# Another table of positions for the attention steps of a fused attention and token-mixing kernel

## The chip, the cores and the metric

One core of a Trainium2 chip runs the whole kernel. The metric is the device time of one execution in microseconds (us); the number given for a kernel is the median of its runs.

## What is computed

The reference has two parts. In the first, for 8 batches and 8 heads, queries are pooled in pairs and attend to 1152 keys; the second mixes the result over tokens and channels:

```python
q_pool = q.reshape(B, H, S // 2, 2, D).mean(axis=3)
scores = scale * np.matmul(q_pool, k.transpose(0, 1, 3, 2))
scores = scores - np.max(scores, axis=-1, keepdims=True)
attn = np.exp(scores)
attn = attn / (np.sum(attn, axis=-1, keepdims=True) + 1e-09)
x = np.matmul(attn, v)            # heads side by side: [8, 576, 512]
theta = x @ w_theta
y = w_tok_r @ (x * cos(theta)) + w_tok_i @ (x * sin(theta))
u = x + y
return u + np.maximum(u @ w_ch, 0.0)
```

All arrays hold float32, the four weight matrices come as 64-bit floats and are taken apart in the kernel.

## The kernel before

The work has two phases. **Phase one** is attention. The 64 (batch, head) problems are done two heads at a time, in 32 *pairs*, numbered 0 to 31. **Phase two** is the mixing, batch by batch, and has an order of its own that the change leaves as it is.

A pair consists of some hundred *steps*, one `Op` each, made in `operations()`. By engine they are:

- SP (DMA issues): `load_q`, `load_k` (four each), `load_v`, `load_max` (six, ten for pair 0), and `norm_spread`, `norm_load`, `norm_save`, `norm_bcast`, `norm_store` for the row sums.
- POOL: `diff` (differences of neighbouring keys, L720) and `ss` (sums of the exponentials, L868).
- DVE: `pool_q` (L713), `t` (two transposes of the operands, L745 and L747; in pair 0 the TensorE does them), `lo` (low parts, L778), `mx` (15 maxima over PSUM, L803), `nm` and `nt` (the row maxima and their transpose, L815 and L818), and `norm_recip`, `norm_out`, `norm_turn` (L920, L944, L949).
- ACT: `hi` (high parts, L774), `rn` (rounds the maxima to `nmrr`, L836), `x` (18 exponentials, L861), `xu` and `sm` (L885, L905).
- PE: `pm` (15 score tiles for the maxima, L791), `e` (18 exact score tiles of three or four terms, L851), `av` (18 products with v, L873), `ns` (row sums, L894).

A step's name is followed here by its two indices, as in the table: `pm40` is the first of the three matmuls of query block 4, `e18` the ninth score tile of the second half of the queries, `av06` the product of the seventh tile of the first half.

What binds the steps is data and room. A block of maxima runs `pm40`, `mx40`, `pm41`, `mx41`, `pm42`, `mx42` in one slot of PSUM; chains of `e` and `x` (up to three tiles, each added onto the one before) hold a slot too; `t` holds one until its `lo` is done. There are four slots of two banks, and `av` and `ns` fill one of them by halves. Exponentials go into 14 buffers, given back once `av` and `ss` (or `ns`) have read them.

The order of all this is made ahead, by a list scheduler (`schedule`, from line 366) that runs on the host. Each step has a *position*, `PLACE[name] + 18 * pair`; entries with the prefix `p0:` replace it for pair 0. Each engine has one list, sorted by position. `ahead` says how many of its first steps may be started out of order: 24 on SP; `LOOK = 8` on the others while the first step in the list belongs to pair 0 or 1, or to the last pair; and one, so the plain sorted order, in all pairs between. Among those it may choose, `look` takes the first in sorted order unless a later one would be finished, by the planner's own durations, before the first could start (plus `slack`):

```python
edge = main[e] and (main[e][0].i < 2 or main[e][0].i >= NPAIRS - 1)
return LOOK if edge else 1
```

A step that has not been run yet, because it waits, keeps its place among the eight. The instructions of each engine are then issued in the order that was found, and on the chip each engine keeps that order.

Beside the pairs runs a second list, 18 weight jobs (`w_fetch` to `w_tlo`), whose position is `w0 + wd * job + wk * step`. On PE a step that needs another array mode than the one before is sorted as if it stood `turn` further back. `early` loads the first input of phase two, and `xhi` and `xlo` split it; `xt` and `th` stand for phase two's first matmuls and issue nothing.

Pair 0 has two sets of maxima: `nm00`, `nt00` and four `load_max` (numbers 0 to 3, L827) give the rows of the first half of the queries and lead over `rn` to its first score tile `e00`; `nm10`, `nt10` and `load_max` 4 to 9 (L827, L833) give the second half, which pair 0 reads from a tile of its own, `nmr_0u`.

Of the kernel before, what the change touches and what calls it, by code (L numbers as in the profile page):

```python
# [25 lines left out]
    "load_k00": -38.40059, "load_k10": -28.36788, "load_k20": -27.61457, "load_k30": -39.35929,  # L26
    "diff00": -32.80156, "diff10": -32.44173, "load_q00": -54.34104, "load_q10": -91.84454,
    "load_q20": -27.44506, "load_q30": -38.99972, "pool_q00": -29.15684, "t10": -22.00105,
    "hi10": -21.02379, "lo10": -20.04949, "t00": -22.18585, "hi00": -22.31522, "lo00": -21.74663,
    "pm40": -17.06847, "mx40": -16.83563, "pm30": -17.17711, "mx30": -18.87555, "pm41": -14.70191,  # L30
    "mx41": -15.31905, "pm31": -14.17544, "mx31": -15.19312, "pm42": -13.57796, "mx42": -15.06456,
    "pm32": -12.76746, "mx32": -14.97779, "pm10": -12.17304, "mx10": -13.89269, "pm00": -11.03266,
    "mx00": -13.56397, "pm11": -9.95283, "mx11": -13.12904, "pm01": -8.94236, "mx01": -12.84205,
    "pm12": -8.45123, "mx12": -12.18622, "pm02": -7.5643, "mx02": -11.83974, "pm20": -7.04275,
    "mx20": -11.61033, "pm21": -6.55952, "mx21": -11.06424, "pm22": -4.02978, "mx22": -9.22241,
    "nm00": -8.00188, "nt00": -6.38411, "load_max00": -24.4908, "load_max10": -24.14235,
    "load_max20": -8.92986, "load_max30": -19.40568, "load_max40": -118.57957,
    "load_max50": -8.27529, "e00": 4.11175, "x00": -1.62783, "e02": 4.64667, "x02": 0.31132,
    "e01": 5.19959, "e04": 5.23843, "x01": 0.32182, "x04": 0.70875, "ss01": 2.41792,
    "e03": 6.0347, "x03": 1.15614, "load_v00": -6.85969, "ss02": 5.42273, "e05": 8.75871,  # L40
    "ss03": 5.61781, "x05": 1.54237, "e06": 9.18085, "x06": 2.58909, "e10": 9.86331,
    "e07": 10.38561, "ss04": 5.9122, "x10": 2.72114, "x07": 2.81716, "e11": 10.43852,
    "e08": 11.21097, "x11": 3.45665, "ss05": 15.96989, "x08": 6.26382, "e13": 11.41578,
    "e12": 11.43369, "x13": 8.12539, "ss06": 16.1637, "x12": 8.88963, "e14": 11.69101,
    "e15": 12.02213, "x14": 11.71284, "av00": 12.31907, "x15": 9.74425, "e16": 15.17488,
    "e17": 15.17109, "av01": 13.07033, "ss11": 7.67054, "x16": 12.96257, "av02": 15.1759,
    "x17": 12.50312, "av10": 16.02034, "av03": 15.34448, "ss12": 8.07714, "av11": 16.18557,
    "av04": 15.38473, "av12": 16.56557, "ss13": 10.54574, "av05": 15.79164, "av13": 17.48058,
    "av06": 16.9326, "av14": 18.02337, "ss14": 11.31074, "av07": 17.89469, "av15": 19.02375,
    "av08": 20.38694, "ss15": 11.52553, "av16": 20.50752, "xu00": 16.19192, "e18": 18.22843,  # L50
    "ss16": 16.35297, "x18": 15.73589, "av17": 21.17044, "av18": 22.34946, "xu10": 17.1598,
    "ns00": 25.06113, "ns10": 25.1094, "ns20": 25.72144, "sm00": 19.45308,
    "norm_spread00": -21.70776, "norm_load00": 13.58894, "norm_recip00": 55.52903,
    "norm_save00": 61.28433, "norm_bcast00": 63.23545, "norm_bcast10": 57.24014,
    "norm_out00": 62.72609, "norm_store00": 31.66353, "norm_turn00": 69.51872,
    "norm_store10": 59.99388, "pool_q10": -107.14221, "ns30": 146.18829, "ns40": -13.08814,
# [1448 lines left out]
```

## Time and profile before

| | us |
|---|---|
| median of 3 runs | 1266.46 (1264.79 to 1267.41) |
| the profiled execution, whole time | 1265.34 |
| its span, first to last instruction | 1263.6 |
| PE busy | 1211.3 |
| DVE busy | 966.7 |
| POOL busy | 810.9 |
| ACT busy | 679.8 |

The span is what the trace shows; the profiled execution's own time is 1.74 us more, for what lies around it. Busy time is time in which an engine has an instruction running, and on PE matmuls overlap. Times in the rows below count from the span's start. Phase one fills the first 817 us or so.

### The profile page before, as it was taken

To read this page: it belongs to the slowest core of one execution; us is meant where nothing else is said; L and a number is where in the kernel's file an instruction comes from. 1 tells how busy PE (TensorE), PEld (TensorE's weight loads), DVE (VectorE), ACT (ScalarE), POOL (GpSimd) and SP (SyncE) were. 2 spreads that over 40 slices of the span, in tenths; PEclk is the share of its full clock that TensorE was granted. 3 is DMA by queue.
4 is the path that set the end of the run, shared out by engine and by line. 5 is a ranking of instruction groups with operands and counts; after the bars stand their busy time and mean duration, and the time that the engine had idled before them with its cause. 6 is when DMAs were issued, how large, how long until landed. Compare 5 with 4: busy or idle time off the path is not lost.

```text
span 1263.6 us, 27774 instructions
## 1 busy us (share of the span) xinstructions
PE 1211.3 (96%) x10915; PEld 946.4 (75%) x10915; DVE 966.7 (77%) x1313; ACT 679.8 (54%) x1129; POOL 810.9 (64%) x596
## 2 busy tenths in 40 slices
PE   3899999999999999999999999999999999999998
PEld 2567666666666766766666666698999999999998
DVE  6788989999888898988989886166675857658553
ACT  1466656656666765666666665464343433344430
POOL 1688988998987998898988888334333423242320
PEclk7899999999999999999999999999999999999999
DMA  6454555557555456455556431315545546455332
GB/s 122 80 105 94 115 102 121 125 124 168 100 86 109 101 107 124 85 101 102 117 98 111 105 68 40 97 34 151 120 110 114 124 110 135 103 121 115 86 52 38
DMA packets 489403, 130.16 MB, mean 103 GB/s; under 512 B 459576, under 2 KB 460280, under 8 KB 489272
## 3 DMA queue, kind: packets, MB, share of 16 engines
q1 hardware_dynamic: 489272, 128.39, 48.9%
q8 instruction: 85, 1.39, 0.5%
q14 instruction: 46, 0.38, 0.1%
HBM read 97.61 MB, written 29.52 MB: 101 GB/s over the span
## 4 chain that ended last, share of the span: by engine, by line
PE 80%; ACT 8%; DVE 6%; DMA 2%; issue 2%; POOL 1%; SPq 0%; ACTq 0%; DVEq 0%; POOLq 0%
PE b L873 23%; PE b L851 18%; PE py L1325 15%; PE b L791 7%; PE pr L1364 6%; ACT pc L861 6%; PE pth L1237 6%; PE b L894 4%; DVE mx L803 2%; DMA xT<-xd 1%; DVE kk L1261 1%; DMA dn<-rod 1%; ACT Z L1294 1%; DVE r L1263 1%; ACT kk L1259 1%
## 5 line engine op out<-in xcount | busy, mean ns | idle before, releaser
L803 DVE TENSOR_REDUCE mx<-b 128x2 f32<-128x768 f32 x480 | 440.3, 953 | 79.4 <-PE b L791 76.7
L868 POOL TENSOR_TENSOR ss<-ss,pc 128x576 f32<-128x576 f32 x314 | 448.7, 1436 | 19.6 <-ACT pc L861 2.6
L861 ACT ACTIVATE pc<-b 128x576 f32<-128x576 f32 x576 | 353.6, 652 | 184.5 <-PE b L851 156.6
L873 PE MATMUL b<-pc,vn 128*64 128x288 f32 x2304 | 306.3, 411 | 0.0
L873 PEld LDWEIGHTS b<-pc,vn 128*64 128x64 f32 x2304 | 154.5, 136 | 112.3 <-issue 17.8
L1325 PE MATMUL py<-wtk,Z 128*128 128x288 f32 x1728 | 234.0, 296 | 0.0
L1325 PEld LDWEIGHTS py<-wtk,Z 128*128 128x128 f32 x1728 | 232.2, 189 | 1.4 <-DVE uT L1341 0.2
L1298 POOL TENSOR_TENSOR Z<-ab,Z 128x512 fp32r<-128x512 f32 x40 | 53.3, 1333 | 266.3 <-ACT Z L1294 266.3
L851 PE MATMUL b<-hi 64*128 64x288 f32 x1152 | 187.1, 321 | 13.2 <-ACT pc L861 8.8
L791 PE MATMUL b<-hi 64*128 64x384 f32 x960 | 172.8, 379 | 14.8 <-DVE mx L803 8.5
L851 PE MATMUL b<-lo,hi 64*128 64x288 f32 x1152 | 170.6, 293 | 0.0
L851 PE MATMUL b<-hi,lo 64*128 64x288 f32 x1152 | 170.2, 292 | 0.0
L868 POOL TENSOR_TENSOR ss<-pc,pc 128x576 f32<-128x576 f32 x64 | 105.5, 1648 | 94.0 <-ACT pc L861 94.0
L851 PEld LDWEIGHTS b<-hi 64*128 64x128 f32 x1152 | 108.3, 185 | 52.8 <-ACT pc L861 33.9
L791 PEld LDWEIGHTS b<-hi 64*128 64x128 f32 x960 | 87.8, 188 | 80.1 <-DVE mx L803 51.9
L851 PEld LDWEIGHTS b<-lo,hi 64*128 64x128 f32 x1152 | 109.1, 186 | 0.0
L851 PEld LDWEIGHTS b<-hi,lo 64*128 64x128 f32 x1152 | 108.8, 185 | 0.0
L1364 PE MATMUL pr<-us,wch 128*128 128x288 f32 x768 | 106.6, 296 | 1.2 <-DVE uT L1377 1.2
L1364 PEld LDWEIGHTS pr<-us,wch 128*128 128x128 f32 x768 | 104.3, 188 | 3.8 <-DVE uT L1377 2.4
L720 POOL TENSOR_TENSOR qk<-qk 128x384 f32<-128x384 f32 x62 | 63.7, 1027 | 20.6 <-DMA qk<-in_k_dram 16.6
L1237 PE MATMUL pth<-wth,xh 128*128 128x512 f32 x288 | 72.9, 395 | 2.4 <-DVE r L1263 2.4
L774 ACT CAST hi<-b 128x768 fp32r<-128x768 f32 x64 | 56.0, 879 | 33.8 <-DVE b L745 23.5
(100 smaller groups left out, 1320.1 us busy)
## 6 DMA issues: line engine op xcount, KB each, us to landing
vn<-in_v_dram SPq DMA_DIRECT2D x32, 576.0 KB
qn<-in_q_dram SPq DMA_DIRECT2D x124, 144.0 KB
qk<-in_k_dram SPq DMA_DIRECT2D x124, 144.0 KB
xd<-xu SPq DMA_DIRECT2D x32, 288.0 KB
xT<-xd SPq DMA_DIRECT2D x8, 1152.0 KB
xn<-xbd SPq DMA_DIRECT2D x140, 64.0 KB
out_dram<-ub SPq DMA_DIRECT2D x124, 72.0 KB
xbd<-xb SPq DMA_DIRECT2D x28, 288.0 KB
```

What stands on the lines that cost most here:

```text
L720: (nc.vector if op.eng == DVE else nc.gpsimd).tensor_tensor(kn[:, c : c + W], kn[:, c : c + W], kn[:, c - W : c], ALU.subtract)
L774: nc.scalar.copy(hi, src)
L791: nc.tensor.matmul(pm[:, h, 0:W], hi[hs, q : q + P], hi[hs, group(g)], start=(g == 0), stop=True, skip_group_check=(g > 0),)
L803: nc.vector.tensor_reduce(maxima(op.i)[:, at, g : g + 1], slots[op.slot][:, :, 0:W], AX.X, ALU.max)
L851: nc.tensor.matmul(pe[:, h, 0:HALF], w[hs], x[hs], start=bool(op.acq and n == 0), stop=(n == len(terms) - 1), skip_group_check=not op.acq,)
L861: nc.scalar.activation(pc, slots[op.slot][:, :, 0:HALF], AF.Exp, scale=SC)
L868: nc.gpsimd.tensor_tensor(st["ss", u], first, st["pc"][u, k], ALU.add)
L873: nc.tensor.matmul(half(op)[hs, 0:HALF], st["vn"][:, h, key(u, k), :], st["pc"][u, k][:, h, :], start=(k == 0), stop=(k == KT - 1),)
L1237: nc.tensor.matmul(th, xs[c][:, j * P : (j + 1) * P], ws[:, c], start=(n == 0), stop=(n == 11))
L1298: engine("zlo", b).tensor_tensor(Z[1], t, Z[0].bitcast(F32), ALU.subtract)
L1325: nc.tensor.matmul(st["py", c, u][:, 0:HALF], Z[zi][:, c * P : (c + 1) * P], wtk[wi][:, kw, u * HALF : (u + 1) * HALF], start=(i == 0 and ...
L1364: nc.tensor.matmul(pr[u][:, 0:HALF], wch[wi][:, c, e * P : (e + 1) * P], st["us", ui][:, c, u * HALF : (u + 1) * HALF], start=(n == 0), st ...
```

## The change

Only the numbers of the table `PLACE` are replaced: every entry but the few that name constants. The steps, their dependences, the durations that the planner assumes, `LOOK`, `CHAINS` and all of phase two's code stay. The entries that the prediction speaks of, in whole lines:

```diff
-    "load_q20": -27.44506, "load_q30": -38.99972, "pool_q00": -29.15684, "t10": -22.00105,
-    "hi10": -21.02379, "lo10": -20.04949, "t00": -22.18585, "hi00": -22.31522, "lo00": -21.74663,
-    "pm40": -17.06847, "mx40": -16.83563, "pm30": -17.17711, "mx30": -18.87555, "pm41": -14.70191,
...
-    "mx00": -13.56397, "pm11": -9.95283, "mx11": -13.12904, "pm01": -8.94236, "mx01": -12.84205,
-    "pm12": -8.45123, "mx12": -12.18622, "pm02": -7.5643, "mx02": -11.83974, "pm20": -7.04275,
...
-    "load_max50": -8.27529, "e00": 4.11175, "x00": -1.62783, "e02": 4.64667, "x02": 0.31132,
-    "e01": 5.19959, "e04": 5.23843, "x01": 0.32182, "x04": 0.70875, "ss01": 2.41792,
-    "e03": 6.0347, "x03": 1.15614, "load_v00": -6.85969, "ss02": 5.42273, "e05": 8.75871,
...
-    "e07": 10.38561, "ss04": 5.9122, "x10": 2.72114, "x07": 2.81716, "e11": 10.43852,
...
-    "av06": 16.9326, "av14": 18.02337, "ss14": 11.31074, "av07": 17.89469, "av15": 19.02375,
-    "av08": 20.38694, "ss15": 11.52553, "av16": 20.50752, "xu00": 16.19192, "e18": 18.22843,
...
-    "norm_spread00": -21.70776, "norm_load00": 13.58894, "norm_recip00": 55.52903,
...
-    "norm_out00": 62.72609, "norm_store00": 31.66353, "norm_turn00": 69.51872,
...
-    "ns50": 7.33146, "slack": 0.1216, "turn": 44.06172, "w0": -1.47751, "wd": 33.05571,
-    "wk": 2.0724, "lk": 1, "early00": 2.50309, "xhi00": 578.18943, "xlo00": 599.84852,
-    "xhi10": 668.31203, "xlo10": 834.59127, "xhi20": 538.26115, "xlo20": 916.41777,
...
-    "p0:nm10": -50.29296, "p0:nt10": -296.24668, "p0:nm00": -68.15714, "p0:nt00": -62.82465,
-    "p0:load_max00": -47.50946, "p0:load_max10": -138.90085, "p0:load_max20": -151.91924,
-    "p0:load_max30": -283.49617, "p0:load_max40": -26.96722, "p0:load_max50": -39.95036,
-    "p0:load_max60": -181.26686, "p0:load_max70": -51.60945, "p0:load_max80": 12.9247,
...
+    "load_q20": -23.94588, "load_q30": -27.22046, "pool_q00": -28.34024, "t10": -23.37827,
+    "hi10": -22.97999, "lo10": -21.41727, "t00": -23.70966, "hi00": -25.07319, "lo00": -23.24259,
+    "pm40": -18.629, "mx40": -17.47197, "pm30": -17.26719, "mx30": -17.15966, "pm41": -14.58323,
...
+    "mx00": -13.81827, "pm11": -9.02264, "mx11": -13.27775, "pm01": -8.705, "mx01": -12.88861,
+    "pm12": -8.31555, "mx12": -11.92126, "pm02": -7.98529, "mx02": -11.19449, "pm20": -7.57071,
...
+    "load_max50": -34.95536, "e00": 3.70511, "x00": -2.06987, "e02": 6.99904, "x02": -1.12835,
+    "e01": 7.42237, "e04": 7.73944, "x01": -1.0359, "x04": -1.01736, "ss01": 0.10044,
+    "e03": 8.32472, "x03": -0.48171, "load_v00": -10.16559, "ss02": 2.50166, "e05": 9.43316,
...
+    "e07": 9.85551, "ss04": 3.55036, "x10": 2.60899, "x07": 2.70415, "e11": 10.52441,
...
+    "av06": 20.10575, "av14": 17.07112, "ss14": 11.50774, "av07": 20.43687, "av15": 19.63034,
+    "av08": 20.88203, "ss15": 15.84528, "av16": 20.24077, "xu00": 15.31038, "e18": 17.80942,
...
+    "norm_spread00": 14.53016, "norm_load00": -7.1203, "norm_recip00": 39.96074,
...
+    "norm_out00": 63.50151, "norm_store00": 32.46633, "norm_turn00": 69.49542,
...
+    "ns50": 8.72092, "slack": 0.12161, "turn": 56.48616, "w0": -3.06778, "wd": 33.18642,
+    "wk": 2.15959, "lk": 1, "early00": 146.82316, "xhi00": 544.88349, "xlo00": 630.17433,
+    "xhi10": 634.75889, "xlo10": 923.38799, "xhi20": 601.46763, "xlo20": 1014.55532,
...
+    "p0:nm10": -3.78377, "p0:nt10": -227.04645, "p0:nm00": -161.15731, "p0:nt00": -23.17844,
+    "p0:load_max00": -88.1277, "p0:load_max10": -119.00684, "p0:load_max20": -225.14677,
+    "p0:load_max30": -155.24402, "p0:load_max40": -98.52721, "p0:load_max50": -9.46839,
+    "p0:load_max60": -112.02231, "p0:load_max70": -47.53628, "p0:load_max80": -9.62434,
```

## Rows read from the trace of the kernel before

**Rows 1.** The page's first part: busy time of each engine

```profile
PE 1211.3 (96%) x10915; PEld 946.4 (75%) x10915; DVE 966.7 (77%) x1313; ACT 679.8 (54%) x1129; POOL 810.9 (64%) x596
```

**Rows 2.** Stretches of the span: busy us of each engine, clock, DMA

```profile
0.00:40.00 40.00, 16.30 (x69) 9.59 (x69) 28.51 (x42) 7.12 (x9) 4.27 (x13) 0.70 0.57 107
...
300.00:400.00 100.00, 98.06 (x1020) 67.15 (x1016) 87.46 (x109) 63.55 (x106) 88.11 (x65) 1.00 0.54 105
...
780.00:820.00 40.00, 36.79 (x365) 23.28 (x366) 9.67 (x17) 18.89 (x36) 20.96 (x15) 1.00 0.22 65
```

**Rows 3.** Stretches of one pair: av of pair 0 to pair 1; sm of pair 10 to 11

```profile
53.24:78.27 25.03, 23.87 (x249) 16.27 (x247) 19.61 (x24) 16.32 (x27) 22.92 (x18) 1.00 0.43 85
...
312.58:336.37 23.79, 23.44 (x248) 16.18 (x250) 20.58 (x25) 14.61 (x24) 22.29 (x17) 1.00 0.55 103
```

**Rows 4.** Timeline of DVE, around pair 0's row maxima

```profile
31.01 0.18 DVE L815 TENSOR_REDUCE nm<-mx 128x10 f32<-128x30 f32 x1
...
31.37 1.15 DVE L747 STREAM_TRANSPOSE b<-qk 128x960 f32<-128x960 f32 x1
```

**Rows 5.** Timeline of SP's queue: pair 0's loads of the row maxima

```profile
31.05 0.65 SPq L827 DMA_DIRECT2D nmrs<-nt  x1
31.82 0.57 SPq L827 DMA_DIRECT2D nmr_0u<-nt  x1
32.45 1.05 SPq L827 DMA_DIRECT2D nmrs<-nt  x2
33.55 0.50 SPq L827 DMA_DIRECT2D nmr_0u<-nt  x1
34.09 0.50 SPq L827 DMA_DIRECT2D nmrs<-nt  x1
```

**Rows 6.** Timeline of ACT, pair 0: rn

```profile
35.67 0.67 ACT L836 CAST nmrr<-nmrs 128x576 fp32r<-128x576 f32 x1 [2.11 <-DMA nmrs<-nt]
```

**Rows 7.** Timeline of PE: a pm step of pair 1, and pair 0's first two e

```profile
37.42 0.69 PE L791 MATMUL b<-hi 64*128 64x384 f32 x2 [0.20 <-DVE mx L803]
37.91 0.44 PE L851 MATMUL b<-hi 64*128 64x288 f32 x2
...
39.84 0.61 PE L851 MATMUL b<-hi 64*128 64x288 f32 x2 [0.46 <-ACT pc L861]
```

**Rows 8.** Stretches of 2 us, where the granted clock (third number from the end) rises

```profile
38.00:40.00 2.00, 1.54 (x14) 1.12 (x10) 1.68 (x3) 0.65 (x1) 0.00 (x0) 0.50 1.04 163
40.00:42.00 2.00, 2.00 (x16) 1.86 (x18) 1.85 (x3) 0.72 (x2) 0.00 (x0) 0.50 1.12 147
42.00:44.00 2.00, 1.78 (x16) 1.50 (x14) 0.87 (x1) 1.59 (x3) 1.34 (x1) 0.69 1.03 218
```

**Rows 9.** Timeline of PE in pair 11: pm02, e11, the block of av, pm30 and pm40

```profile
315.24 0.34 PE L791 MATMUL b<-hi 64*128 64x384 f32 x2
315.72 0.41 PE L851 MATMUL b<-hi 64*128 64x288 f32 x2
...
321.22 5.56 PE L873 MATMUL b<-pc,vn 128*64 128x288 f32 x44
...
327.20 0.51 PE L791 MATMUL b<-hi 64*128 64x384 f32 x4
```

**Rows 10.** Timeline of DVE, the same stretch: five maxima, then both lo

```profile
312.93 4.64 DVE L803 TENSOR_REDUCE mx<-b 128x2 f32<-128x768 f32 x5
...
325.12 1.16 DVE L778 TENSOR_TENSOR lo<-b,hi 128x960 fp32r<-128x960 f32 x1 [0.18 <-ACT hi L774]
```

**Rows 11.** Timeline of ACT, the same stretch: the second hi

```profile
324.12 0.96 ACT L774 CAST hi<-b 128x960 fp32r<-128x960 f32 x1 [0.26 <-DVE b L747]
```

**Rows 12.** Groups by line over the whole span: the transposes of the weight jobs

```profile
L1093 PE MATMUL b<-ident,ws 128*128 128x128 f32 x32 | 5.1, 281 | 2.7 <-DVE mx L803 2.3 <-POOL ss L868 0.4
```

**Rows 13.** Timeline of DVE at the end of phase one: the last xlo

```profile
809.27 1.56 DVE L605 TENSOR_TENSOR xl<-xT,xh 128x640 fp32r<-128x640 f32 x2
```

**Rows 14.** Chain of waits: where phase two's first matmuls begin

```profile
817.75 0.66 PE pxn L1212 x4
```

40 rows, old and new, of the table PLACE are left out of this document.

## The prediction

> **What bounds the kernel now.** I read the page first, then the stretches, then the timelines of single engines. The page has PE busy for 96% of the span [rows 1], so a gain must come from stretches where PE is not. The stretches say where these are: of the first 40 us PE is busy for 16.30, in 100 us in the middle for 98.06, and in the 40 us that end phase one for 36.79 [rows 2]. So there are some 23.7 us without matmuls at the start, about 2% in the pairs, and 3.2 us at the end of phase one. An ordinary pair lasts 23.79 us with 0.35 us of idle PE; the one from pair 0 to pair 1 lasts 25.03, with 1.16 idle [rows 3]. In the first 40 us the mean granted clock is 0.70 [rows 2]; narrower stretches show 0.50 until 42 us and 0.69 in the two after that, so a rise to 1.00 at 43.2 ((0.69 - 0.50) / 0.50 of 2 us before 44) [rows 8]. So pair 0's first score tiles run at the lower of the clock's two levels, 1.2 instead of 2.4 GHz.
>
> **Part A, the start of pair 0.** In the old order DVE does `nm10` (and its `nt10`) before pair 1's second transpose `t10` [rows 4]. In the table of before `p0:nm10` stands at -50.3; now it is at -3.78, behind pair 1's `t10` (-23.38 + 18 = -5.38) and `lo00` (-5.24), and sorted order decides among steps that can start. So I expect `t10` where `nm10` was: 0.36 us earlier (31.37 to 31.01), and with it `hi10` and pair 1's first `pm`. The second set of maxima then comes behind, and its loads behind the first set's. In the old order two of them (31.82 and 33.55) stand between the four loads that `rn` needs, the last of which is issued at 34.09 [rows 5]. Without them it is issued 0.63 us (31.82 to 32.45) and 0.54 us (33.55 to 34.09) earlier, 1.17 us, at about 32.9. `rn` started 1.58 us after that issue (35.67 against 34.09) [rows 5, 6]; at the same distance it starts at 34.5 and ends at 35.2. The old `e00` was put behind `pm` steps of pair 1, the last at 37.42, and began at 37.91, 1.57 us after `rn` had ended at 36.34 [rows 6, 7]. In the new table it moves up from 4.11 to 3.71, while pair 1's `pm42` goes back from 4.42 to 6.31 (the table's number plus 18): the step at 37.42 need no longer be in front of it. Once `rn` is done at 35.2 and the `pm` then on PE, of 0.69 us, has ended, it should start, about 36.0: 1.9 us earlier. What is late next is the chain `e00`, `x00`, `e02`, whose second link came 1.93 us after the first [rows 7]. Not all 1.9 us survive: in the first 5 us PE runs at the lower clock, where work moved forward takes twice the time. I take -1.5, with 0 (the DVE, which still has 15 maxima of 0.93 us [rows 10] and pair 1's operands to make, sets the pace) and -1.9 as ends.
>
> The Trainium skill ("DMA: Bandwidth & Descriptors", its cost model of a transfer) gives every transfer a fixed cost of about 2 us. The 1.58 us from issue to `rn` above is less. By the page `rn` would start at 34.9 instead of 34.5 and the part would be worth -1.1 instead of -1.5.
>
> **Part B, from pair 0 to pair 1.** This stretch holds 1.24 us more than an ordinary pair [rows 3], and here the planner may still choose among eight steps. New positions can give any part of it back, or take as much again; nearest are the ordinary pairs, in which the sorted order already runs at 23.79. I take half, -0.6, with ends -1.2 and +0.6.
>
> **Part C, pairs 2 to 30.** Sorted by position, the two tables give nearly one order. PE has these differences: `pm01` before `e05`, `pm20` before `e11`, `av13` and `av14` ahead and `av06`, `av07` back, and `pm40` before `e18`. The first two cost and save nothing: `e11` waits for `x10` until 315.72, with `pm20` behind it [rows 9]; `pm20` needs the slot that `mx12` frees, the third of five maxima of 0.93 us that follow each other from 312.93, so at 315.7 [rows 10]. It then runs in the gap and pushes `e11` back by about its own 0.3 us; `e08`, behind both in either table, stays where it was. The third matters. The block of av is now 9 steps (36 of its 44 instructions: 4.5 of 5.5 us), so `pm40` stands at 321.22 + 4.5 = 325.7 [rows 9]. It needs `hi10`, done at 325.08: 0.6 us to spare [rows 11]. `pm30` follows `e18`, which filled the 0.5 us between the old block's end and 327.20 [rows 9]; with `pm40` itself 0.2 it comes at 326.4, and needs the slot of `t10`, free when `lo10` ends at 326.28 [rows 10]: 0.1 us to spare. A DVE step of a weight job put in between, as in some pairs it must be, makes PE wait. Against that `norm_turn` goes behind `lo10`, which helps its four pairs. ACT's `rn` before `x18`, POOL's `diff` among `ss`, `norm_recip` a pair earlier: each keeps a cover, since what they feed is used on PE a microsecond or more later; without it they would count toward the upper end. I take +0.6 for all 29 pairs (0.1 us in six of them), with -1.0 and, at 0.2 us in each, +6 as ends.
>
> **Part D, the rest.** SP's queue gets new positions for all its loads, but it may look 24 steps ahead, and between pairs its loads wait for data, not for each other: nothing, with two issues of 0.5 us [rows 5] either way as ends. The weight jobs' transposes of the common form take 5.1 us of PE over the span, plus waits of 2.7 us [rows 12]; `turn` at 56 instead of 44 and `w0`, `wd` move them by a pair at most: 0, with -2.7 and +2.7 as ends. At the end of phase one the splits of `xhi`, `xlo` are done on DVE by 810.8, and their matmuls begin at 817.75 [rows 13, 14], so their positions are covered by 6.9 us. Pair 31 may again be reordered among eight: 0, with -1.5 and +1.5 out of 3.2 us idle [rows 2].
>
> **The sum.** -1.5 - 0.6 + 0.6 + 0 = -1.5 us. Against the profiled execution's own 1265.34 this makes 1263.8; that execution is 1.12 below the median of the runs shown, so I predict the median as 1266.46 - 1.5 = 1265.0. A measurement of this kernel can tell about 0.2%, or 2.5 us, from no change, so this is a small gain inside what counts as the same.
>
> **Rivals.** *The start opens wider.* The clock rises earlier because PE's work begins earlier, and pairs 0 and 1 lose all their idle time. Price: the 3.4 us of work between 39.84 and 43.2 run at the higher clock save 1.7 us, part A gives its whole 1.9 and part B its 1.2: -4.8, or 1261.7. For it: PE goes over to the higher clock after it has been busy throughout 40 to 42 [rows 8]. Against it: 1.54 of 2 us busy in 38 to 40 were followed by no rise [rows 8], and the gaps of the first chain remain.
> The Trainium skill ("TensorE: Matmul & The Clock Gate", Part 1) has the low clock as the idle state, which sustained matmul activity ends. By that rule the rise moves with the start of steady work, which is this rival's first term; the rows above agree in kind.
>
> *PE waits for the operands in every pair.* `pm40` and `pm30` now stand 1.7 and 0.8 us earlier (the two of them ran from 327.20 on, `pm30` first), against 0.6 and 0.1 us to spare (part C). If the new place loses 0.2 us in each of 29 pairs, 5.8 - 1.5 - 0.6 = +3.7 us: 1270.2. It decides from the point at which `lo10` ends more than 0.1 us later against the av block than in rows 9 and 10. For it: DVE is busy for 20.58 of 23.79 us [rows 3] and weight steps fall anywhere. Against it: in the pair shown both are ready.
>
> *The change moves nothing that sets the end.* In pairs 2 to 30 it is the same order but for a few swaps, and at the start DVE's 15 maxima of pair 1 may decide when pair 0's tiles can go on. Then 1266.5.
>
> **How the numbers follow.** Small gain 0.38 (1265.0; its own range is 1264.0 to 1266.4), wider start 0.34, waits in every pair 0.16, nothing 0.12. So faster by over 0.2% is 0.34, within it 0.50, slower 0.16. The range reaches to the wider start at 1261.6 and, for waits in some pairs only, up to 1268.2; it leaves out most of the slower rival and a little beneath the faster one.
>
> **What would show it.** Right: in DVE's timeline pair 1's long transpose ahead of `nm10`; four `nmrs` loads in a row on SP; `rn` near 34.5 and `e00` near 36.0; the first block of av between 50.5 and 52.5 instead of at 53.24; ordinary pairs of 23.8 us. The rise of the clock shows whether the wider start holds: at 43 as now, or near 40. Wrong: pairs of 24.0 us or more with PE idle in front of `pm40` or `pm30`; or `e00` early and the av block where it was.

## The result, and the profile after

The changed kernel takes **1272.76 us** (median of 6 runs, 1270.46 to 1275.26), the kernel before beside it 1265.64 (6 runs, 1264.61 to 1267.41): 1.0053 of it, 95% interval 1.0041 to 1.0066. It is slower by 7.1 us, and 4.6 us above the range that was predicted. The profiled execution took 1274.46 us, its span is 1272.7.

The first view splits the span into four stretches: up to pair 1's `sm` (the ACT step that ends a pair, L905), pairs 2 to 29, pairs 30 and 31, and phase two. Columns: stretch, its length, then busy time of PE, PEld, DVE, ACT, POOL with counts, granted clock, DMA share, GB/s. First the kernel before:

```profile
0.00:95.56 95.56, 68.64 (x589) 45.45 (x591) 73.75 (x95) 40.70 (x65) 51.88 (x49) 0.86 0.55 104
95.56:771.77 676.21, 663.01 (x6930) 456.70 (x6932) 597.40 (x732) 434.54 (x724) 593.12 (x429) 1.00 0.53 107
771.77:817.19 45.42, 42.26 (x446) 27.98 (x446) 16.49 (x27) 23.73 (x44) 27.34 (x20) 1.00 0.14 41
817.19:1263.56 446.37, 437.43 (x2954) 416.23 (x2954) 279.05 (x459) 180.87 (x298) 138.52 (x100) 1.00 0.46 103
```

and the changed one:

```profile
0.00:94.00 94.00, 69.51 (x589) 46.45 (x591) 74.12 (x96) 40.73 (x64) 51.91 (x48) 1.00 0.60 104
94.00:777.33 683.33, 670.78 (x6930) 460.23 (x6932) 592.69 (x732) 434.77 (x725) 591.37 (x430) 1.00 0.54 106
777.33:821.72 44.39, 42.29 (x446) 28.09 (x446) 16.00 (x26) 23.64 (x45) 27.40 (x20) 1.00 0.17 46
821.72:1272.68 450.96, 438.17 (x2954) 417.21 (x2954) 281.48 (x459) 181.03 (x298) 139.02 (x100) 0.99 0.46 102
```

(The 1.00 in the first line of the changed kernel measures nothing: in this profile the clock's record begins only with its rise at 45.8 us. The step of `pm` shown below at 37.49 takes 0.69 us, as at the lower level in [rows 7].)

The start gains 1.6 us, the last two pairs 1.0. The 28 pairs between lose **7.1**, and phase two, whose code is the same, lasts 4.6 longer. PE's busy time in the 28 pairs grows by 7.8 us for the same 6930 matmuls, so most of the loss doesn't show as idle PE. (The profile models where a matmul ends, so a wait of some 0.3 us or less can count as busy.) The groups by line show where it is. Of PE's two groups of score tiles in that stretch (`pm` is L791, `e`'s first term L851; columns: busy, mean ns of one, idle before and its releaser), before:

```profile
L851 PE MATMUL b<-hi 64*128 64x288 f32 x1008 | 161.5, 317 | 8.0 <-ACT pc L861 4.1
L791 PE MATMUL b<-hi 64*128 64x384 f32 x842 | 147.4, 368 | 0.6 <-DVE mx L803 0.5
```

after:

```profile
L851 PE MATMUL b<-hi 64*128 64x288 f32 x1008 | 161.3, 317 | 4.4 <-ACT sm L905 0.7 <-ACT pc L861 0.2
L791 PE MATMUL b<-hi 64*128 64x384 f32 x842 | 154.3, 385 | 3.8 <-DVE mx L803 2.0
```

`pm` is 6.9 us longer busy (385 instead of 368 ns a matmul) and waits 3.2 us more, while the wait in front of `e` falls by 3.6. Read together they show a trade: in the old order PE waited a little for exponentials in front of `e`; now `pm` stands in those gaps, more often alone, and waits itself. In pair 11 `pm40` and `pm30` take 0.44 and 0.36 us apart from each other, and 0.51 together before [rows 9].

Pair by pair, the time from `sm` to `sm` in the changed kernel is 23.86 to 23.90 us in most ordinary pairs (23.79 before, [rows 3]); 0.2 to 0.5 more than before in seven of the eight with a `w_turn` (pair 6: 25.35 for 24.87) and in pair 15; and in three pairs that were ordinary before far more: 16 with 24.71, 24 with 24.87, 25 with 25.02. Pair 11, in the changed kernel:

```profile
311.72:335.62 23.90, 23.68 (x248) 16.31 (x250) 19.13 (x24) 14.60 (x24) 21.74 (x17) 1.00 0.58 98
```

Lines that answer to those shown of before. DVE at the start, for [rows 4]:

```profile
31.43 1.15 DVE L747 STREAM_TRANSPOSE b<-qk 128x960 f32<-128x960 f32 x1
...
33.35 0.16 DVE L815 TENSOR_REDUCE nm<-mx 128x10 f32<-128x30 f32 x1
```

SP's queue, for [rows 5], with the two loads issued just ahead:

```profile
29.66 0.84 SPq L729 DMA_DIRECT2D vn<-in_v_dram  x1
30.54 0.58 SPq L670 DMA_DIRECT2D qn<-in_q_dram  x1
31.57 2.37 SPq L827 DMA_DIRECT2D nmrs<-nt  x4
```

ACT's `rn`, for [rows 6]:

```profile
36.46 0.67 ACT L836 CAST nmrr<-nmrs 128x576 fp32r<-128x576 f32 x1 [2.83 <-DMA nmrs<-nt]
```

and PE's step of pair 1 with `e00` behind it, for [rows 7]:

```profile
37.49 0.69 PE L791 MATMUL b<-hi 64*128 64x384 f32 x2 [0.19 <-DVE mx L803]
37.97 0.44 PE L851 MATMUL b<-hi 64*128 64x288 f32 x2
```

The reordering is as forecast (the long transpose ahead of `nm10`, four `nmrs` loads in a row), yet `rn` comes at 36.46 and `e00` at 37.97, no earlier than before.

### The profile page after: what moved, and what is told of

It is laid out like the page before. It is cut to its first block, busy times and chain, and to the rows that moved or that the text cites. A ratio compares the mean times of both kernels' runs of the same rounds, so it can differ in the third digit from the quotient of the medians.

```text
span 1272.7 us, 27808 instructions
## 1 busy us (share of the span) xinstructions
PE 1220.8 (96%) x10915; PEld 952.0 (75%) x10915; DVE 964.3 (76%) x1313; ACT 680.2 (53%) x1129; POOL 809.7 (64%) x596
## 4 chain that ended last, share of the span: by engine, by line
PE 72%; DVE 13%; ACT 7%; DMA 3%; POOL 2%; issue 2%; SPq 1%; ACTq 0%; DVEq 0%; POOLq 0%
PE b L873 19%; PE b L851 16%; PE py L1325 14%; PE b L791 7%; PE pr L1364 6%; PE pth L1237 5%; DVE mx L803 5%; PE b L894 4%; ACT pc L861 3%; DMA xT<-xd 2%; POOL ss L868 1%; DVE lo L778 1%; DVE kk L1261 1%; DVE b L747 1%; DMA dn<-rod 1%
## 5 line engine op out<-in xcount | busy, mean ns | idle before, releaser
L868 POOL TENSOR_TENSOR ss<-ss,pc 128x576 f32<-128x576 f32 x314 | 449.6, 1439 | 19.1 <-ACT pc L861 3.0
L791 PE MATMUL b<-hi 64*128 64x384 f32 x960 | 180.7, 397 | 18.0 <-DVE mx L803 9.7
L851 PE MATMUL b<-hi 64*128 64x288 f32 x1152 | 186.9, 321 | 7.0 <-ACT pc L861 2.3
L851 PE MATMUL b<-lo,hi 64*128 64x288 f32 x1152 | 170.7, 293 | 0.0
L851 PE MATMUL b<-hi,lo 64*128 64x288 f32 x1152 | 170.3, 292 | 0.0
L791 PEld LDWEIGHTS b<-hi 64*128 64x128 f32 x960 | 87.5, 190 | 106.6 <-DVE mx L803 62.0
L851 PEld LDWEIGHTS b<-hi 64*128 64x128 f32 x1152 | 108.5, 185 | 29.3 <-ACT pc L861 18.6
L851 PEld LDWEIGHTS b<-lo,hi 64*128 64x128 f32 x1152 | 109.4, 187 | 0.0
L851 PEld LDWEIGHTS b<-hi,lo 64*128 64x128 f32 x1152 | 108.8, 186 | 0.0
L778 DVE TENSOR_TENSOR lo<-b,hi 128x768 fp32r<-128x768 f32 x64 | 66.9, 1047 | 10.1 <-ACT hi L774 9.9
```

What stands on the lines that cost most here:

```text
L778: nc.vector.tensor_tensor(lo, src, hi.bitcast(F32), ALU.subtract)
L791: nc.tensor.matmul(pm[:, h, 0:W], hi[hs, q : q + P], hi[hs, group(g)], start=(g == 0), stop=True, skip_group_check=(g > 0),)
L851: nc.tensor.matmul(pe[:, h, 0:HALF], w[hs], x[hs], start=bool(op.acq and n == 0), stop=(n == len(terms) - 1), skip_group_check=not op.acq,)
L868: nc.gpsimd.tensor_tensor(st["ss", u], first, st["pc"][u, k], ALU.add)
```

## The experiments

Eleven runs; with the first profiles of before and after the table has thirteen profiled executions, split as above (us). "Clock" is where the granted clock rises to 1.00 at the start, "falls" counts the stretches of phase two in which it goes back to 0.50, 1.2 GHz. The column of pairs 2 to 29 repeats to 0.6 us between executions of one kernel. The kernel before, run again beside each set of runs, had medians from 1265.3 to 1267.1 us, so runs of different sets are compared by their ratio to it.

| kernel | clock | to `sm` of pair 1 | pairs 2-29 | pairs 30, 31 | phase two | falls |
|---|---|---|---|---|---|---|
| before | 43.2 | 95.56 | 676.21 | 45.42 | 446.37 | 0 |
| before_again | 45.7 | 96.12 | 676.16 | 45.43 | 448.34 | 1 |
| after | 45.8 | 94.00 | 683.33 | 44.39 | 450.96 | 1 |
| after_again | 46.6 | 94.24 | 682.76 | 44.40 | 449.59 | 2 |
| after_pm_back | 43.0 | 92.86 | 679.47 | 44.42 | 450.71 | 1 |
| after_w_back | 44.1 | 93.84 | 680.91 | 44.41 | 448.25 | 1 |
| after_v0_late | 44.4 | 92.57 | 683.42 | 44.40 | 448.36 | 1 |
| after_e00_first | 39.7 | 93.87 | 683.29 | 44.36 | 448.42 | 1 |
| after_av11 | 41.8 | 92.80 | 690.57 | 44.40 | 449.02 | 1 |
| before_pm40_early | 43.2 | 94.03 | 683.04 | 45.45 | 452.01 | 2 |
| new_start | 41.4 | 92.50 | 676.04 | 45.44 | 447.42 | 0 |
| new_rest | 43.9 | 95.32 | 682.71 | 44.39 | 448.56 | 1 |
| new_start_v_late | 43.2 | 92.72 | 675.93 | 44.39 | 449.90 | 1 |

Where an edit moves steps, they are moved in the planner's finished order (`behind` and `ahead` put a step next to another one); all else keeps its place. Only `before_pm40_early` changes the table, and there the planner makes a new order. Lines added to a kernel shift the line numbers of the rest, so that `pm` is L791 in one and L813 in another.

**after_again** is the changed kernel without an edit.

> The changed kernel itself, once more, for what of its time is the execution's and not the change's. In the two profiles the part after the last ns sum is 451.0 us after the change and 446.4 before it, although no step there was changed. Theory (these 4.6 us belong to the one execution): the new profile shows that part at 446 to 449 us, without the fall of the granted clock to 0.50 at 882 us, while pairs 1 to 31 repeat to 0.3 us; the time is 1272.8 +- 1.5. Rival (the change sets something off that stays in phase two): the part is 450.5 to 451.5 again, with the fall at the same place.

Measured: 1272.77 us (5 runs), 1.0052 of before, interval 1.0038 to 1.0066. Phase one repeats but for pair 24 (24.32 us for 24.87; the other pairs from 2 to 29 are within 0.03), phase two gives 449.59, between the two expectations, with a fall of the clock at the same place and a second one later.

**before_again**, the kernel before without an edit.

> The kernel of before once more, for its part after the last ns sum: 446.4 us in its first profile, 448.2 to 451.0 in five profiles of kernels made from the changed one, although that part is the same code. One transfer of xT, issued about 274 us into that part, ends 5.1 us after its issue in the first and 6.3 to 6.5 us in the five. Theory (where phase two falls against the transfers and the code loads depends on the kernel before it, and repeats): again 446.4 +- 0.7 us and 5.1 us. Rival (each execution draws its own): the part is above 448 us, or that transfer takes over 6 us.

Measured: phase two in 448.34 us, so the rival holds, though the xT transfer again took 5.1 us. (The kernel as a whole was timed once, at 1267.82 us.) The same wait and the same eight matmuls of phase two, in the first profile of before and in this one:

```profile
877.73 2.11 PE L1237 MATMUL pth<-wth,xh 128*128 128x512 f32 x8 [2.14 <-DVE r L1263]
```

```profile
878.26 3.54 PE L1237 MATMUL pth<-wth,xh 128*128 128x512 f32 x8 [2.14 <-DVE r L1263]
```

One program, one wait of 2.14 us, and the clock falls after it in one execution and not in the other: 1.4 us for these eight matmuls, of which 0.8 us are left in the start of later matmuls. Of the thirteen profiles the two without a fall have the shortest phase two (446.4, 447.4), the two with two falls 449.6 and 452.0; the nine with one fall lie between 448.3 and 451.0, so something else is drawn as well. The waits of DVE show it. For the input xT (columns: total, times, longest) it waits in phase two, before and after:

```profile
DVE xT L1194 <- DMA xT<-xd: 5.0, 5, 1.1
DVE xT L1194 <- DMA xT<-xd: 8.8, 5, 3.3
```

These are 3.8 us more, and with the 0.8 us that a fall left above they make up the 4.6. In the other eleven profiles the waits for xT sum to 5.6 to 8.1 us. The three longest phase twos (450.7, 451.0 and 452.0, in after_pm_back, after and before_pm40_early) are the three in which DVE waits 2.8 to 3.3 us for the xT that it takes up some 226 us into phase two; in the other ten that wait is 0.8 to 1.0. What makes the transfer late was not tried. So this part is drawn anew by each execution; it is the part in which two profiles of one kernel differ by 1.4 to 2.0 us.

**after_pm_back**: the `pm01` and `pm20` swaps undone.

```diff
+    for i in range(2, NPAIRS - 2):
+        ahead(find("e", i, 0, 5), find("pm", i + 1, 0, 1))
+        ahead(find("e", i, 1, 1), find("pm", i + 1, 2, 0))
```

> In pairs 2 to 29 pm01 goes back behind e05, and pm20 behind e11; nothing else moves. Theory (these two swaps, which the prediction costed at nothing, cost 0.08 us in every pair): ordinary pairs last 23.79 to 23.81 us instead of 23.87 to 23.90, and the whole kernel 28 x 0.08 = 2.2 us less than the changed one, 1270.6. Rival (the 0.08 comes from pm40's new place or from the DVE's order): ordinary pairs stay at 23.87 to 23.90 and the time at 1272.8.

Measured: 1268.31 us (11 runs), 1.0024 of before (1.0014 to 1.0034), 4.5 us under after_again. Ordinary pairs are 23.78 to 23.82 long: 0.09 less, as the theory says, 2.5 us in 28 pairs. In pair 11 the first `av` behind the swaps starts 6.35 us after `sm`, as before the change, and 6.44 with them. Pair 16 becomes regular as well (23.79 for 24.71), unlooked for. The weight step `w_sign` (`wf<-raw,wf`), which takes 1.89 us there in the changed kernel (shown under after_w_back), takes 0.69 here:

```profile
445.83 0.69 DVE L1057 SCALAR_TENSOR_TENSOR wf<-raw,wf 128x513 uint32<-128x513 uint32 x1
```

The traces say why. Of the 234 `w_sign` of the thirteen profiles, 74 start while an instruction of POOL that began over 0.03 us earlier has more than 0.22 us to run; each of these ends 0.55 to 0.62 us after that instruction and takes 0.82 to 2.00 us. The other 160 take 0.63 to 0.82. In pair 16 of the changed kernel an `ss` on POOL starts 0.07 us ahead of `w_sign`; here the next `ss` starts 0.05 us behind it. The stall hung on a tenth of a microsecond. Of the 4.5 us, pairs 2 to 29 hold 3.3 by the profiles, and the start of this one is 1.4 earlier, with an earlier rise of the clock.

**after_w_back**: weight steps moved in three pairs.

```diff
+    for m, i in ((9, 18), (14, 27)):
+        job = {o.name: o for o in order if o.i == -1 - m}
+        behind(job["w_shift"], job["w_max"])
+        ahead(job["w_sign"], job["w_mask"])
+    behind(job["w_abs"], find("x", 25, 0, 6))
+    ahead(job["w_low"], job["w_abs"])
```

> Three weight steps of two jobs change place: in pairs 16 and 25 the shift goes back to right behind its max, and the sign stands behind the maxima mx40 and mx30 instead of ahead of one of them; in pair 24 ACT takes low and abs of a job (they wait for its fetch) after sm and two tiles of the next pair instead of ahead of sm. Theory (the irregular pairs are weight steps that stand in front of a step for which PE waits): pair 16 falls from 24.71 to 23.9 us, pair 24 from 24.87 to 23.9, pair 25 from 25.02 to 23.9, in all 2.9 us, and the time to 1269.9. Rival (what these steps wait for is late anyway, so the stall moves with them): the pairs, or their neighbours 17 and 26, keep 2 us or more of it, and the time is above 1271.5.

Two places of the changed kernel show what it is about. In pair 16, PE and DVE:

```profile
448.19 3.13 PE L873 MATMUL b<-pc,vn 128*64 128x288 f32 x24
452.02 0.62 PE L791 MATMUL b<-hi 64*128 64x384 f32 x4 [0.70 <-DVE mx L803]
...
447.63 0.68 DVE L1031 TENSOR_SCALAR wf<-ws 128x513 uint32<-128x513 uint32 x1
448.34 1.89 DVE L1038 SCALAR_TENSOR_TENSOR wf<-raw,wf 128x513 uint32<-128x513 uint32 x1
450.15 1.81 DVE L803 TENSOR_REDUCE mx<-b 128x2 f32<-128x768 f32 x2
```

Two steps of a weight job, 2.5 us, 1.2 of them because `w_sign` stands for POOL, come between `lo10` and the first maxima; the next `pm` needs the slot that those free. In pair 24, ACT and PE:

```profile
652.90 0.72 ACT L1019 ACTIVATE raw<-raw 128x576 f32<-128x576 uint32 x1 [1.62 <-DMA raw<-in_moe_w_tok_r_dram]
653.53 0.48 ACT L905 ACTIVATE sm<-b,eps 128x288 f32<-128x288 f32 x1
...
654.06 0.40 PE L851 MATMUL b<-hi 64*128 64x288 f32 x2 [0.69 <-ACT sm L905]
```

ACT waits 1.62 us for a weight fetch, `sm` stands behind it, and PE behind `sm`. Measured: 1270.31 us (5 runs), 1.0043 (1.0028 to 1.0058). Pair 16 falls to 23.93 and 24 to 23.80, but 25 only to 24.60, since ACT's two weight steps now delay exponentials there and PE waits for them:

```profile
655.41 0.40 PE L873 MATMUL b<-hi 64*128 64x288 f32 x2 [0.44 <-ACT pc L883]
```

That is 2.3 of the 2.9 us expected against the first profile of the changed kernel, and 1.7 against after_again: pair 24, which waits for a fetch, takes 24.2 to 25.1 in the six profiles that have its order. The theory holds but for that new place.

**after_av11**: the block of `av` in front of `pm40` as long as before.

```diff
+    for i in range(2, NPAIRS - 2):
+        pm = find("pm", i + 2, 4, 0)
+        for k in ((1, 5), (0, 6)):
+            av = find("av", i, *k)
+            if order.index(pm) < order.index(av):
+                ahead(av, pm)
```

> In pairs 2 to 29 of the changed kernel av15 and av06 go back ahead of pm40, so that pm40, e18 and pm30 follow 11 steps of av as before the change; nothing else moves. Theory (in the pairs with a w_turn pm30 stands 0.2 to 0.3 us ahead of the end of lo10, the wait that the prediction's slower rival named): pairs 6, 12, 14, 19, 21, 26, 28 lose 0.25 to 0.35 us each, some 2 us in all, ordinary pairs stay at 23.87 to 23.90, and the time is 1270.7. Rival (these pairs are longer because of DVE's weight steps, wherever PE's block ends): they stay within 0.1 us of 25.35, 25.05, 25.29, 25.19, 25.35, 25.11, 25.34.

The wait that the theory meant, in pair 6 of the changed kernel: `pm40`, `e18`, `pm30` on PE, and DVE's two `lo`, done at 205.99:

```profile
200.58 4.59 PE L873 MATMUL b<-pc,vn 128*64 128x288 f32 x36
205.10 0.44 PE L791 MATMUL b<-hi 64*128 64x384 f32 x2
205.38 0.30 PE L851 MATMUL b<-hi 64*128 64x288 f32 x2
...
206.04 0.44 PE L791 MATMUL b<-hi 64*128 64x384 f32 x2
...
203.84 2.15 DVE L778 TENSOR_TENSOR lo<-b,hi 128x768 fp32r<-128x768 f32 x2
```

Measured: the opposite of a gain, 1279.62 us (4 runs), 1.0104 (1.0090 to 1.0118). That wait is gone, but pair 6 takes 25.44, and pairs 2, 8, 10, 17 and 23, ordinary before, 0.8 to 1.3 us more each. PE's waits in pairs 2 to 29 point to the reason:

```profile
PE b L813 <- DVE mx L825: 11.0, 16, 1.4
```

against 2.0 us in three waits in the changed kernel. DVE's order expects `pm40` early; with the `av` ahead it comes a microsecond later (14.22 instead of 13.24 us into pair 11), and where a weight step stands among the maxima, the next `pm` waits for them. PE's place for `pm40` and DVE's for `mx40` can't be set singly, and this run doesn't price the first alone.

**before_pm40_early**: the same part from the other side, three positions in the old table.

```diff
-    "pm40": -17.06847, "mx40": -16.83563, "pm30": -17.17711, "mx30": -18.87555, "pm41": -14.70191,
+    "pm40": -17.8, "mx40": -16.83563, "pm30": -17.17711, "mx30": -18.87555, "pm41": -14.70191,
...
-    "av06": 16.9326, "av14": 18.02337, "ss14": 11.31074, "av07": 17.89469, "av15": 19.02375,
+    "av06": 20.3, "av14": 18.02337, "ss14": 11.31074, "av07": 20.35, "av15": 19.02375,
```

The planner's new order differs from the old one in more than these three steps: on DVE the shifts of eleven of the 18 weight jobs and some signs and masks move, most of the shifts from ahead of `mx30` and `mx40` to behind them, and on ACT the first two steps of two weight jobs come earlier. DVE keeps `mx30` ahead of `mx40`, where the changed kernel has `mx40` first. So this run is no clean test of PE's swaps.

> The kernel of before with three new positions alone, so that pm40 stands ahead of e18 and av06, av07 behind it, in all pairs: the part of the change that the prediction's slower rival was about. Theory (it costs only where a w_turn makes lo10 late): ordinary pairs stay at 23.79, each of the w_turn pairs gains 0.2 to 0.4 us, in all about 2 us, and the time is 1267.3. Rival 1 (it costs in every pair): ordinary pairs 23.95 to 24.0, over 1269.5. Rival 2 (it costs nothing): 1265.3 +- 1.

Measured: 1275.24 us (5 runs), 1.0058 (1.0044 to 1.0072). Ordinary pairs stay at 23.80, so rival 1 falls; seven of the pairs with a `w_turn` take 0.1 to 0.4 us more, 1.75 in all, near the 2 of the theory. But pairs 7 to 10 take 0.2 to 0.35 us more, 22 takes 25.70, 23 24.75 and 29 25.03: pairs 2 to 29 in all 6.8 us, not 2. In pairs 7 to 10 the old order has `norm_turn` ahead of `lo10`, and `pm30` starts 0.05 us after `lo10`'s end; the changed table, as part C of the prediction says, puts `norm_turn` behind it. In pair 22 a weight step that the planner has moved ahead of `sm` waits on ACT for its fetch, and PE behind `sm`, the mechanism of pair 24 above:

```profile
605.00 0.67 ACT L1019 ACTIVATE raw<-raw 128x513 f32<-128x513 uint32 x1 [2.58 <-DMA raw<-in_moe_w_ch_dram]
...
606.11 0.40 PE L851 MATMUL b<-hi 64*128 64x288 f32 x2 [1.59 <-ACT sm L905]
```

The start, on the other hand, gains 1.5 us by it: pair 1 takes 23.80 us instead of 25.11.

**after_v0_late**: one DMA issue moved.

```diff
+    behind(find("load_v", 0), find("load_k", 1, 1))
```

> The load of pair 0's v goes behind the loads of pair 1, as it stood before the change, so that the weight fetch and pair 1's loads are issued first. Theory (the load of v ahead of them made the start 0.5 us late): the weight fetch is issued at 3.6 instead of 5.2 us, the first lo begins at 13.7 instead of 14.24, e00 at 37.4 to 37.5 instead of 37.97, sm of pair 0 at 69.5 instead of 70.07, and the time is 0.5 us less than the changed kernel's. Rival (the start is set by the loads of q and k, which stand ahead in both): first lo and e00 stay within 0.1 us of 14.24 and 37.97.

SP's first issues and ACT's first instruction in the changed kernel:

```profile
2.75 2.43 SPq L729 DMA_DIRECT2D vn<-in_v_dram  x1
5.22 0.47 SPq L1009 DMA_DIRECT2D raw<-in_moe_w_theta_dram  x1
```

and with the load moved:

```profile
3.67 1.54 SPq L1026 DMA_DIRECT2D raw<-in_moe_w_theta_dram  x1
...
10.11 1.28 ACT L1036 ACT_TABLE_LOAD   x1 [10.11 <-DMA raw<-in_moe_w_theta_dram]
```

Measured: 1271.16 us (5 runs), 1.0043 (1.0031 to 1.0056). ACT starts with a weight step, so it waits for the fetch: until 10.11 us here, 11.4 to 12.3 in the seven profiles with the load of v first, 9.9 to 11.0 in the six without. First `lo` at 12.79, `e00` at 36.53, pair 1's `sm` at 92.57: 1.4 us earlier than after, three times what was expected. One profile can't price the move: in new_start_v_late, below, it brings the first `lo` 0.4 us forward (13.67 for 14.07 in new_start), and pair 1's `sm` comes 0.2 us later (92.72 for 92.50), with a later rise of the clock.

**after_e00_first**: pair 1's load of v later, `e00` ahead of `pm42`.

```diff
+    behind(find("load_v", 1), find("load_q", 2, 2))
+    ahead(find("e", 0, 0, 0), find("pm", 1, 4, 2))
```

> Two moves at the start of the changed kernel: the load of pair 1's v goes behind the maxima's loads and pair 2's k and q, and e00 of pair 0 stands ahead of pair 1's pm42. Theory (rn was late behind that load, and e00 behind pm42): rn starts 1.5 us after the last of its four loads is issued instead of 2.0 to 2.6 us, e00 starts at 37.3 to 37.6 instead of 37.97 to 38.24, and sm of pair 0 comes 0.5 us earlier than 70.1 to 70.3; the time is 0.5 us less. Rival (DVE's maxima of pair 1 set the pace, not e00): e00 is earlier and sm of pair 0 stays within 0.2 us.

```profile
32.27 2.37 SPq L846 DMA_DIRECT2D nmrs<-nt  x4
...
35.73 0.67 ACT L855 CAST nmrr<-nmrs 128x576 fp32r<-128x576 f32 x1 [1.42 <-DMA nmrs<-nt]
...
37.77 0.44 PE L870 MATMUL b<-hi 64*128 64x288 f32 x2
```

Measured: 1270.34 us (7 runs), 1.0026 (1.0015 to 1.0037). `rn` starts 1.1 us after the four issues end (35.73 against 34.64), as in the kernel before, and 2.5 in after (36.46 against 33.94), so the load of v in front of them did hold them up (1.8 to 2.9 in the seven other profiles that have it there). Here the whole start ran late: against the first `lo` (14.93, 14.24 in after) `e00` is 0.9 us earlier. It still comes 1.4 us after the end of `rn`, behind six matmuls of `pm` that had waited for DVE's maxima until 36.42. `sm` of pair 0 comes 55.0 us behind the first `lo`, inside the 54.5 to 55.8 of the eight other profiles with the new start, so a gain of the 0.5 us expected can't be told from their spread. That fits the rival; that the maxima set the pace was not tried by itself. By its ratio the kernel is 0.26% faster than after_again (1.0026 against 1.0052, intervals that do not meet), but its profile has nothing of that in phase one (821.52 us, 821.72 and 821.41 in the two of the changed kernel); where it comes from is not shown.

**new_start** and **new_rest** splice the two orders.

```diff
+def spliced():
+    runs = [schedule(operations(), t) for t in (OTHER, PLACE)]
+    given = {}
+    for e in range(5):
+        other, own = ([o for o in run if o.eng == e] for run in runs)
+        at = [0, len(own)]
+        for cut in (85,):
+            at.insert(-1, min(
+                k for k in range(len(own))
+                if other[k].begin >= cut and {o.n for o in other[:k]} == {o.n for o in own[:k]}
+            ))
+        for n, (a, b) in enumerate(zip(at, at[1:])):
+            for k in range(a, b):
+                given[(own if n % 2 else other)[k].n] = k
+    return schedule(operations(), PLACE, given)
```

`OTHER` is the table for the beginning; with `given`, the planner only places the steps in the order found.

> Every engine's steps in the order of the changed kernel up to the middle of pair 1, and in that of the kernel before from there on. So far the last ns sum came at 817.2 and 817.7 us before and at 821.7 and 821.4 after the change, that of pair 1 at 95.6 and 96.1 against 94.0 and 94.2. Theory (the first two pairs give 1.7 us and pairs 2 to 31 take 5.9): pair 1's ns sum at 94.1, ordinary pairs of 23.79, the last ns sum at 815.7, and the time 1.7 us less than that of the kernel before. Rival (what the start gains is lost at the seam, since the next pairs' operands are no earlier): pair 2 or 3 is longer by a microsecond or more, the last ns sum is not under 817, and the time is that of the kernel before.

> The counterpart: the order of the kernel before up to the middle of pair 1, and the changed one from there on. Theory: pair 1's ns sum at 95.8, ordinary pairs of 23.87 to 23.90, irregular pairs near 16, 24 and 25, the last ns sum at 95.8 + 727.5 = 823.3, and the time 6 us or more over that of the kernel before, the slowest of the four combinations. Rival (the long pairs of the changed kernel come from its start, which sets when DVE and PE meet): pairs 16, 24 and 25 are regular, and the last ns sum is under 821.

Measured: new_start 1265.59 us (11 runs), 0.9985 of before (0.9973 to 0.9997); new_rest 1271.9 (9 runs), 1.0041 (1.0027 to 1.0054). Pairs 2 to 29 of new_start, and PE's `pm` in them:

```profile
92.50:768.54 676.04, 663.11 (x6930) 456.95 (x6932) 595.51 (x732) 435.22 (x724) 593.74 (x429) 1.00 0.52 107
```

```profile
L854 PE MATMUL b<-hi 64*128 64x384 f32 x842 | 147.6, 369 | 0.5 <-DVE mx L866 0.3
```

and of new_rest:

```profile
95.32:778.03 682.71, 670.60 (x6930) 460.31 (x6932) 592.79 (x732) 434.84 (x724) 591.36 (x430) 1.00 0.54 106
```

```profile
L854 PE MATMUL b<-hi 64*128 64x384 f32 x842 | 154.2, 384 | 3.8 <-DVE mx L866 2.0
```

Both theories hold for pairs 2 to 31: nothing is lost at the seam, and the irregular pairs (16 with 24.74, 24 with 24.42, 25 with 25.03) belong to the order of the rest, not to the start. There each half does what its source does, within 0.7 us. The times do not add up so well: the starts came 1.6 us (new_start) and 0.5 (new_rest) earlier than expected, new_rest is 5.0 us over the kernel before and not 6 or more, and -1.3 and +5.0 by the medians make 3.7 of the whole change's 7.1.

**new_start_v_late** has cuts at 85 and 750, so that the last two pairs take the changed order too, and the move of after_v0_late.

> The order of the changed kernel up to the middle of pair 1 with the load of pair 0's v behind the loads of pair 1, that of the kernel before in the middle, and the changed order again for the last two pairs. Theory (each part does alone what it did in the whole): first lo at 12.8 to 13.2 us, pair 1's ns sum at 92.6, pairs 2 to 29 as before (676.2 in all), the last two 44.4 instead of 45.4, the last ns sum at 813.2, and the time 4.2 us less than that of the kernel before, 0.9967 of it. Rival (phase two takes the gain back, as it added some 3 us to most kernels with the changed order): the last ns sum at 813.2, but the time within 2 us of the kernel before.

Measured: **1263.9 us** (11 runs) against 1266.9 of before, 0.9975 of it (0.9964 to 0.9985): faster than both kernels. Phase one ends at 813.04, as expected. The first `lo` came at 13.67, late for this start: the fetch, issued at 2.76, took until 10.99. Some of the gain is missing: 3.0 us by the medians instead of 4.2, between the two expectations; in the profile it is phase two, 449.90 us, that takes it.

## Why the prediction was wrong

**The term that failed is part C**, pairs 2 to 30: +0.6, with an end of +6; it measured +7.1 in pairs 2 to 29 (new_rest alone: 6.5). (Pair 30 is 2.9 us shorter and pair 31 1.9 longer; together they give the -1.0 of the last stretch, for which part D had 0, with 1.5 either way. Counted to the `sm` of pair 30, part C is +4.2.) Three sentences made it too small.

- "The first two cost and save nothing." The swaps of `pm01` and `pm20` cost 0.09 us in each of 28 pairs, 2.5 us (after_pm_back). `pm20` does fill the gap in front of `e11`, but PE comes out of that stretch 0.09 us later (6.44 for 6.35), and [rows 9] show only that `e11` waited, not what the chain behind it could bear.
- "0.1 us to spare" for `pm30`. In ordinary pairs it was enough, and their block is no longer than before (before_pm40_early, 23.80). In the eight pairs with a `w_turn` and in pair 15 `pm30` stood until `lo10` was done (206.04 against 205.99 in pair 6). That is the mechanism of the slower rival, at its own turning point, in nine pairs and not in 29. Elsewhere `pm30` starts 0.13 us after the last matmul of `e18` does; what it starts later than that sums to 1.3 us in the eight pairs. Seven of them are together 1.9 us longer than before in after_pm_back, and 1.75 in before_pm40_early, which moves weight steps too. So the wait is seen for 1.3 of some 1.8 us; no run prices it alone.
- "A DVE step of a weight job put in between, as in some pairs it must be, makes PE wait" was counted with 0.1 us in six pairs, and part D took the weight jobs' new places for 0. Three pairs, 16, 24 and 25, lost 2.9 us, because 2.5 us of DVE steps or a fetch not yet landed stood where 0.1 to 0.6 us were to spare; after_w_back takes 1.7 to 2.3 of that back. In 16 and 25 the long step is a `w_sign` held up by POOL (1.89 and 1.86 us for 0.7), a cost that the prediction doesn't name; and pair 16's share goes whether the weight steps or the swaps are put back.

Together 2.5 + 1.8 + 2.9 = 7.2, for the 7.1; the first and the last are shown by runs, the middle one partly by the trace alone. Part C's list of what differs also leaves out `pm31`, now ahead of `pm41`, and on DVE `mx40`, now ahead of `mx30`; no run prices these.

**Part A and B** came out near their sum by luck. Forecast -2.1 for the first two pairs; measured -1.6 and -1.9 in the two pairs of profiles, and more in most profiles with the new start. But between the boundaries of [rows 3], the first `av` of pair 0 and of pair 1, A gave 4.0 us (49.24 for 53.24, ahead of the 50.5 to 52.5 named as a sign) and B lost 2.3 (27.32 for 25.03), each outside its range. Counted to the `sm` of each pair, A gave 0.4 and B 1.2 (pair 1 fell from 25.11 to 23.94). The start of `av` thus said little about the end of the pair. Part A's chain failed in two links. `rn` did not start at 34.5, since the load of pair 1's v now goes out just ahead of the four loads. And `e00` would have been bound in any case by the `pm` steps of pair 1: the step at 37.42 in [rows 7] was `pm32`, not `pm42`, which stood behind `e00` in the old order and which the planner now puts in front of it. An issue that part D costed at nothing, pair 0's v ahead of the weight fetch, came on top: the first `lo` starts at 14.0 to 14.9 us in the seven profiles with it and at 12.8 to 13.7 in the six without. What B gained has a source that the prediction looked at in part C alone: with the three positions of before_pm40_early, and the rest of the table as before, pair 1 takes 23.80 us.

By the Trainium skill ("DMA: Bandwidth & Descriptors", its cost model of a transfer), with a fixed cost of about 2 us, `rn` was to be later than by the row of before. It was, but by more, and the traces do not bear out one fixed figure: with the load of v in front `rn` began 3.0 us after the start of the last issue (36.46 against 33.44), without it, in after_e00_first, 1.6, as in the row of before. The page fits its figure to transfers that GpSimd issues; these are issued by SP.

**The sum** left phase two out, as code that isn't touched. By the medians it holds the other 3 us of the 7.1 (phase one by two profiles each: 817.45 to 821.56, +4.1: -1.7 in the first two pairs, +6.8 in pairs 2 to 29, -1.0 in the last two). Each execution draws it, and the draw shows as falls of the clock and as waits for xT; but a draw alone needn't differ between two sets of runs, and whether the changed order makes either likelier stays open. Long waits for xT came with the old table as well (before_pm40_early), and new_rest, with the changed pairs, took 5.0 us more than before and its phase one 5.0.

**The rivals.** "The start opens wider" has B's 1.2 us right if counted from `sm` to `sm`, but its clock term didn't come: the rise was at 45.8, not near 40. (In the nine profiles with the new start it lay between 39.7 and 46.6, in the four with the old one between 43.2 and 45.7.) "PE waits for the operands in every pair" was the right side for a part of the right reason. That the pairs would be 24.0 us or more was named as the sign of error; it showed in the irregular pairs, while the ordinary ones moved by 0.09.

## What to carry to other kernels

A swap that fills a gap on the bounding engine is not free by that alone; what counts is when the engine comes out of the stretch behind the gap. Here 0.09 us in each of 28 pairs was a third of the loss. When an order written by a planner repeats with a second, slower rhythm beside it (18 jobs on 32 pairs), look at the pairs where the two meet, not at the ordinary one: margins of 0.1 to 0.6 us hold in the ordinary pair and fail in others. A new position in a planner's table is not a swap of two steps: before reading its result, compare the whole orders. And parts of a new order can be kept or refused by splicing where all engines have done the same set of steps: the stretches of pairs 2 to 29 and of the last two pairs then repeated to within 0.7 us, while the start and phase two moved from one execution to the next.

## What the runs showed of the hardware

The granted clock's rise at the start moves between executions of one program (43.2 and 45.7 us before, with `e00` at 37.91 and 37.90). After one and the same wait of 2.14 us it fell to 0.50 in one execution and not in the next, 1.4 us in the eight matmuls behind it, of which 0.8 us are left later. Between these two profiles the later rise goes with 0.6 us at pair 1's `sm`, so a difference of 1 us and more between two single profiles can be the clock's alone.

A `w_sign` on DVE that starts while an instruction of POOL is running ends 0.55 to 0.62 us after that instruction does, in all 74 cases of thirteen profiles with more than 0.22 us of it left; it then takes up to 2.00 us instead of 0.63 to 0.82. An `ss` that starts 0.05 us behind a `w_sign`, as in pair 16 of after_pm_back, doesn't hold it up. (The profile's spans on POOL are rough, but the 74 agree to 0.07 us.)
